# Low parts of the weights on DVE instead of POOL, and three more turns in a routing phase

## The chip, the cores and the metric

One core of a Trainium2 chip. The metric is the device time in microseconds of one execution; the number given is the median of several.

## What is computed

The reference chains three parts on float32 data.

```
state_t = gamma_h * state_{t-1} + k_t v_t^T          # per batch and head, 768 steps
y_t = (q_t . state_t) / sqrt(64)                     # decayed linear attention, 4 x 8 heads
x = y as 3072 tokens x 512
logits = x @ w_gate                                  # 8 experts, at most 384 tokens each
for (token, e) by falling logit:                     # greedy, over all 24576 pairs
    if token is free and expert e has room: assign
h = relu(x[e's tokens] @ w1[e]) @ w2[e]              # 512 -> 1024 -> 512
out = softplus(h @ w_in) @ w_out                     # 512 -> 2048 -> 512
```

The assignment is exact: which token goes to which expert depends on the order of all logits.

## The kernel before

The order of the instructions on each engine is written out by hand: each engine runs its instructions in the order in which the program emits them, and waits on the others by semaphores.

Up to about 203 us `Attn` computes the attention in 24 chunks of 128 tokens, and `Conv` turns the second network's weights, kept as 64-bit numbers, into float32 parts on DVE. Then `Ffn.start` runs routing phase 0, and `Ffn.emit` the feed-forward work of eight experts.

**Matmuls.** Every float32 product is made of three matmuls on rounded high parts and low parts: high times high, low times high, high times low (`mm3`). So each operand is split. `split_w` (L599) splits a 128x512 weight tile: ScalarE copies `raw` to `whi` with rounding (L604), and L605 subtracts it from `raw`, which gives `wlo`. There are 256 such tiles, 128 from `wraw` (w1 and w2 of the chosen experts, loaded by SP's queue) and 128 from `wo`. `whi` and `wlo` have rings of six buffers, `weights` (L788) keeps four tiles ahead of their use. Activations are split on ScalarE and DVE: `h1h`/`h1l` (L611, L612), `x2h`/`x2l` (L614, L615), `gh`/`gl` (L696, L697).

**Steps.** `plan` (L734) lists the steps of an expert: eight M1 (first layer, a block of 128 of 1024 hidden units, twelve matmuls), eight M2 (second layer), sixteen F1 (first layer of the second network), sixteen F2, and three `xt`, which transpose the next expert's token rows. M1, M2 and F1 have twelve matmuls 384 columns wide, F2 nine of 512. An F1 ends in three ScalarE operations (`sp`) and `gf` on DVE (L683); the `gl` made from it is needed two steps later by F2.

**Turns.** Routing goes expert by expert: phase i (`Route.phase`, L393) finds the expert that is filled next and the list of its tokens, and runs beside the matmuls of the experts before it. It is a generator; each `yield` ends a turn. `emit` (L767) calls for every step `weights`, then the step, then, on every step while the next list isn't there, else on every second one, one turn by `route` (L804). A phase starts with `top` (L354), which takes for each token its best remaining expert. Then come three levels of 46, 46 and 32 thresholds, each counted twice (coarse, fine): `compare` on DVE makes `G` (L378), two turns later `count` (L383) adds it up by 24 small matmuls (L385), DVE makes `ind` of it (L431), one turn later TensorE spreads it (L437), and DVE makes `satj` and the next base from that (L440, L446). Behind the levels come the counts `rs` (L457, used two turns later by the matmul of L464), the expert's number (turn "expert"), one-hot tiles `ohq` (L511) that begin with `tot` (L492), and the token list (turn "list"). If F1 with f = 10 comes before the next list is there, the loop at L779 runs all missing turns at once. `fetch_x` (L626) then gathers the next expert's rows by DMAs that POOL issues.

**Start.** In `start` (L816) the first two weight tiles are split in the turn of the first `ohq` of phase 0, the next two right behind the list.

Of the kernel before, what the change touches and what calls it, by code (L numbers as in the profile page):

```python
# [9 lines left out]
FT = mybir.dt.float32  # L10
# [6 lines left out]
OP = mybir.AluOpType  # L17
# [263 lines left out]
class Route:  # L281
# [72 lines left out]
    def top(self, c0, c1, first):  # L354

        v, E, n = self.nc.vector, self.E, c1 - c0
        s = slice(c0, c1)
        lm, m, aed, ik, sg = self.lm[:, s], self.m[:, s], self.aed[:, s], self.ik[:, s], self.sg[:, s]
        src = self.L[:, s]
        if not first:  # L360
            v.tensor_tensor(lm, src, self.pen[:, None, :].to_broadcast([128, n, E]), op=OP.add)
            src = lm
            v.tensor_scalar(self.u[:, s], self.asg[:, s], 0.0, None, op0=OP.is_equal)
        v.tensor_reduce(m, src, axis=AX.X, op=OP.max)
        v.tensor_tensor(lm, src, self.bc(m, n, E), op=OP.is_equal)
        v.tensor_scalar(m, m, 0.0, None, op0=OP.add)
        v.tensor_tensor(lm, lm, self.desc[:, None, :].to_broadcast([128, n, E]), op=OP.mult)
        v.tensor_scalar(sg, m.bitcast(I32), 31, 0x7fffffff, op0=OP.arith_shift_right, op1=OP.bitwise_and)
        v.tensor_reduce(aed, lm, axis=AX.X, op=OP.max)
        v.tensor_tensor(ik, m.bitcast(I32), sg, op=OP.bitwise_xor)  # L370
        v.tensor_tensor(self.oe[:, s], lm, self.bc(aed, n, E), op=OP.is_equal)
        v.tensor_scalar(sg, ik, 21, None, op0=OP.arith_shift_right)
        v.scalar_tensor_tensor(self.kf[:, s], sg, 1025.0, self.u[:, s], op0=OP.add, op1=OP.mult)
        v.tensor_scalar(self.kx[:, s], self.bc(self.kf[:, s], n, 2), -1.0, None, op0=OP.add)
# [12 lines left out]

    def first_part(self, c0, c1):

        self.top(c0, c1, True)  # L390
        self.compare(c0, c1, self.t0, 46)

    def phase(self, i, slow=True):  # L393
        nc, N, E, w = self.nc, self.N, self.E, self.wp
# [2 lines left out]
        gap = range  # L397
        last = i == E - 1
        if i:
            self.top(0, N, False)  # L400
        base = self.zero
        ps = None
        if last:
# [1 line left out]
        for l, (J, s1, sh, span) in enumerate(() if last else LEVELS):  # L405
            if l:
                lo = T([128, N], I32, "lo")
# [159 lines left out]
class Ffn:  # L567
# [31 lines left out]
    def split_w(self, key):  # L599
        nc = self.nc  # L600
        raw = self.wout[key[2]] if key[0] == "wo" else self.raws.pop(key)
        hi = self.ring.tile([128, 512], FR, name="whi")
        lo = self.ring.tile([128, 512], FR, name="wlo")
        nc.scalar.activation(hi, raw, AF.Copy)  # L604
        nc.gpsimd.tensor_sub(lo, raw, hi.bitcast(FT))  # L605
        self.ws[key] = hi, lo

    def split_act(self, ps, hi, lo, relu=False):
# [303 lines left out]
```

## Time and profile before

| what | us |
|---|---|
| median of three runs | 1120.59 (1120.57 to 1124.83) |
| the profiled execution | 1123.62 |
| its span (first to last instruction) | 1121.5 |
| TensorE busy | 1020.8 |
| DVE busy | 689.1 |
| ScalarE busy | 535.1 |
| POOL busy | 442.3 |

The page lists busy times by engine and by line of code; PE is TensorE, PEld its weight loads, ACT ScalarE. A row of a timeline gives the start of an instruction from the span's start, its duration, engine, line and operands, and in brackets the idle time before it with what ended that. Instructions of an engine may overlap by their start-up, so a row's duration can be somewhat longer than its distance to the next row.

### The profile page before, as it was taken

What the parts mean: (1) busy time and instruction counts of PE and PEld (TensorE: products, weight loads), DVE (VectorE), ACT (ScalarE), POOL (GpSimd) and SP (SyncE); (2) the same over time, 40 slices, a digit from 0 to 9 for tenths busy, and PEclk for the clock granted to TensorE, in tenths of its full rate; (3) what the DMA queues carried; (4) which work ended last, traced back from release to release, by engine and by line L of the source; (5) the groups of instructions that cost most, each with busy time, mean ns of one, the idle gap of its engine ahead of it and who ended that gap; (6) DMA issues with size and microseconds to landing.
All of it is one profiled execution on the core that took longest, in us unless ns stands there. A gap on an engine that the chain in (4) does not pass through costs nothing.

```text
span 1121.5 us, 18513 instructions
## 1 busy us (share of the span) xinstructions
PE 1020.8 (91%) x7041; PEld 922.8 (82%) x7041; DVE 689.1 (61%) x1510; ACT 535.1 (48%) x1041; POOL 442.3 (39%) x386
## 2 busy tenths in 40 slices
PE   5877874489999999999999999999999999999997
PEld 5776763378878988898889888988888899989996
DVE  5999999755765656467646665865586622441332
ACT  2444332224554465436543654365536654664663
POOL 4323320333335424542355235523452454337422
PEclk9888886589999999999999999999999999999999
DMA  8887873320113201320122012301220222013000
GB/s 317 302 284 263 301 228 104 104 75 1 39 38 105 65 1 38 95 75 1 39 81 90 1 38 76 94 1 30 75 67 1 76 85 85 1 47 122 1 1 29
DMA packets 38873, 97.51 MB, mean 87 GB/s; under 512 B 5120, under 2 KB 5248, under 8 KB 38784
## 3 DMA queue, kind: packets, MB, share of 16 engines
q1 hardware_dynamic: 34128, 83.11, 23.1%
q0 software_dynamic: 3840, 12.59, 3.4%
q8 instruction: 55, 0.90, 0.3%
q10 hardware_dynamic: 816, 0.63, 0.2%
q14 instruction: 34, 0.28, 0.1%
HBM read 83.73 MB, written 12.58 MB: 86 GB/s over the span
## 4 chain that ended last, share of the span: by engine, by line
PE 68%; DVE 23%; issue 3%; ACT 2%; DMA 2%; POOL 1%; SPq 0%; ACTq 0%; POOLq 0%; DVEq 0%
PE h L619 11%; PE h L621 10%; PE h L620 10%; PE acc L717 8%; PE acc L719 7%; PE acc L718 7%; PE acc L619 3%; PE acc L621 3%; PE acc L620 3%; PE rt L385 2%; DVE at L121 2%; DVE cM L233 2%; DVE cX L247 2%; DVE cX L251 2%; DVE base L446 1%
## 5 line engine op out<-in xcount | busy, mean ns | idle before, releaser
L605 POOL TENSOR_TENSOR wlo<-wo,whi 128x512 fp32r<-128x512 f32 x128 | 169.2, 1327 | 357.9 <-ACT whi L604 325.4
L605 POOL TENSOR_TENSOR wlo<-wraw,whi 128x512 fp32r<-128x512 f32 x128 | 164.1, 1302 | 189.6 <-ACT whi L604 172.3
L683 DVE SCALAR_TENSOR_TENSOR gf<-h,sp 128x384 f32<-128x384 f32 x128 | 71.2, 557 | 179.0 <-ACT sp L681 178.9
L619 PE MATMUL h<-x2h,wih 128*128 128x384 f32 x512 | 176.8, 345 | 0.0
L621 PE MATMUL h<-x2l,wih 128*128 128x384 f32 x512 | 173.2, 338 | 0.2 <-DVE x2l L615 0.2
L620 PE MATMUL h<-x2h,wil 128*128 128x384 f32 x512 | 173.4, 339 | 0.0
L717 PE MATMUL acc<-whi,gh 128*128 128x512 f32 x384 | 154.8, 403 | 0.0
L719 PE MATMUL acc<-whi,gl 128*128 128x512 f32 x384 | 152.5, 397 | 2.2 <-DVE gl L697 2.2
L718 PE MATMUL acc<-wlo,gh 128*128 128x512 f32 x384 | 152.0, 396 | 0.0
L679 ACT ACTIVATE sp<-h 128x384 f32<-128x384 f32 x128 | 62.4, 488 | 150.3 <-PE h L621 148.9
L697 DVE TENSOR_TENSOR gl<-gf,gh 128x384 fp32r<-128x384 f32 x128 | 103.4, 807 | 39.9 <-ACT gh L696 39.8
L611 ACT ACTIVATE h1h<-h 128x384 fp32r<-128x384 f32 x64 | 31.4, 491 | 170.7 <-PE h L621 170.7
L612 DVE SCALAR_TENSOR_TENSOR h1l<-h,h1h 128x384 fp32r<-128x384 f32 x64 | 35.3, 555 | 115.6 <-ACT h1h L611 115.6
L619 PEld LDWEIGHTS h<-x2h,wih 128*128 128x128 f32 x512 | 96.1, 188 | 4.1
L620 PEld LDWEIGHTS h<-x2h,wil 128*128 128x128 f32 x512 | 96.2, 188 | 3.0
L621 PEld LDWEIGHTS h<-x2l,wih 128*128 128x128 f32 x512 | 96.1, 188 | 0.8 <-DVE x2l L615 0.8
L619 PE MATMUL acc<-h1h,whi 128*128 128x384 f32 x256 | 89.7, 350 | 0.0
L719 PEld LDWEIGHTS acc<-whi,gl 128*128 128x128 f32 x384 | 72.4, 189 | 21.0 <-DVE gl L697 4.3
L619 PE MATMUL h<-xh,whi 128*128 128x384 f32 x256 | 89.0, 348 | 0.7 <-ACT xh L614 0.7
L696 ACT ACTIVATE gh<-gf 128x384 fp32r<-128x384 f32 x128 | 67.1, 524 | 46.5 <-DVE gf L683 39.0
L621 PE MATMUL acc<-h1l,whi 128*128 128x384 f32 x256 | 87.4, 341 | 0.0
L620 PE MATMUL acc<-h1h,wlo 128*128 128x384 f32 x256 | 87.2, 341 | 0.0
(197 smaller groups left out, 2047.4 us busy)
## 6 DMA issues: line engine op xcount, KB each, us to landing
wraw<-in_moe_w_dram SPq DMA_DIRECT2D x128, 256.0 KB, 2.7
qk_t<-in_qk_dram SPq DMA_DIRECT2D x24, 512.0 KB, 6.8
kv_t<-in_kv_dram SPq DMA_DIRECT2D x24, 512.0 KB, 5.5
raw<-in_moe_w_in_dram SPq DMA_DIRECT2D x16, 512.0 KB, 5.3
raw<-in_moe_w_out_dram SPq DMA_DIRECT2D x16, 512.0 KB, 4.7
xd<-xs SPq DMA_DIRECT2D x24, 256.0 KB, 6.0
gqt<-in_gqt_dram SPq DMA_DIRECT2D x5, 256.0 KB, 6.6
ctab<-in_tab_dram ACTq DMA_DIRECT2D x1, 536.0 KB, 5.7
```

The lines of the kernel that those rows point to most:

```text
L605: nc.gpsimd.tensor_sub(lo, raw, hi.bitcast(FT))
L612: nc.vector.scalar_tensor_tensor(lo, ps, 0.0, hi.bitcast(FT), op0=OP.max, op1=OP.subtract)
L619: nc.tensor.matmul(ps, wh, ah, start=start, stop=False)
L620: nc.tensor.matmul(ps, wl, ah, start=False, stop=False)
L621: nc.tensor.matmul(ps, wh, al, start=False, stop=stop)
L679: nc.scalar.activation(a, ps, AF.Abs)
L683: nc.vector.scalar_tensor_tensor(g, ps, 0.0, a, op0=OP.max, op1=OP.add)
L696: nc.scalar.activation(gh, g, AF.Copy)
L697: nc.vector.tensor_tensor(gl, g, gh.bitcast(FT), op=OP.subtract)
L717: nc.tensor.matmul(ps, gh[:, s], wh, start=f == 0, stop=False)
L718: nc.tensor.matmul(ps, gh[:, s], wl, start=False, stop=False)
L719: nc.tensor.matmul(ps, gl[:, s], wh, start=False, stop=f == 15)
```

## The change

The subtraction that makes `wlo` is issued on DVE instead of POOL, at the same place of the program. And `top` becomes a generator: for the phases in the loop it ends a turn behind the masked logits, a second one behind the best expert's index, and `phase` ends a third one behind `top`, ahead of the first `compare`. Phase 0's `first_part` runs it through without turns.

```diff
@@ top
             v.tensor_scalar(self.u[:, s], self.asg[:, s], 0.0, None, op0=OP.is_equal)
+            yield
         v.tensor_reduce(m, src, axis=AX.X, op=OP.max)
...
         v.tensor_reduce(aed, lm, axis=AX.X, op=OP.max)
+        if not first:
+            yield
         v.tensor_tensor(ik, m.bitcast(I32), sg, op=OP.bitwise_xor)
@@ first_part
-        self.top(c0, c1, True)
+        for _ in self.top(c0, c1, True):
+            pass
@@ phase
         if i:
-            self.top(0, N, False)
+            yield from self.top(0, N, False)
+            yield
@@ split_w
         nc.scalar.activation(hi, raw, AF.Copy)
-        nc.gpsimd.tensor_sub(lo, raw, hi.bitcast(FT))
+        nc.vector.tensor_tensor(lo, raw, hi.bitcast(FT), op=OP.subtract)
```

## Rows read from the trace of the kernel before

**Rows 1.** the head of the page: busy time, share of the span, instructions of each engine.

```profile
PE 1020.8 (91%) x7041; PEld 922.8 (82%) x7041; DVE 689.1 (61%) x1510; ACT 535.1 (48%) x1041; POOL 442.3 (39%) x386
```

**Rows 2.** the span cut into stretches: busy time of PE, PEld, DVE, ACT, POOL; clock; DMA.

```profile
216.00:320.00 104.00, 96.13 (x618) 87.13 (x619) 63.20 (x145) 44.84 (x88) 37.12 (x29) 0.93 0.14 41
...
880.00:1100.00 220.00, 220.00 (x1184) 205.41 (x1183) 78.43 (x122) 124.64 (x243) 97.40 (x84) 1.00 0.16 48
```

**Rows 3.** whom TensorE waited for, 216 to 880 us: total, times, longest.

```profile
PE rt L385 <- DVE G L378: 11.1, 7, 4.9
PE rt L464 <- DVE rs L457: 3.6, 3, 1.6
PE acc L719 <- DVE gl L697: 2.2, 3, 1.1
```

**Rows 4.** the stretches of low granted clock, in the same columns.

```profile
227.20:234.10 6.90, 4.23 (x34) 4.15 (x34) 3.86 (x9) 0.00 (x0) 1.49 (x2) 0.51 0.29 88
...
264.80:268.20 3.40, 3.40 (x12) 2.96 (x11) 1.55 (x4) 1.47 (x3) 0.00 (x0) 0.50 0.00 0
...
322.80:326.20 3.40, 3.11 (x29) 2.64 (x30) 2.60 (x6) 0.05 (x1) 1.26 (x1) 0.50 0.26 63
```

**Rows 5.** groups by line and shape: count, busy us, mean ns, idle time before.

```profile
L605 POOL TENSOR_TENSOR wlo<-wo,whi 128x512 fp32r<-128x512 f32 x128 | 169.2, 1327 | 357.9 <-ACT whi L604 325.4 <-PE acc L718 13.1 <-PE rt L437 10.9
...
L697 DVE TENSOR_TENSOR gl<-gf,gh 128x384 fp32r<-128x384 f32 x128 | 103.4, 807 | 39.9 <-ACT gh L696 39.8
...
L446 DVE TENSOR_TENSOR base<-ksat 128x1 f32<-128x1 f32 x21 | 23.1, 1099 | 0.7
...
L260 DVE TENSOR_TENSOR wo<-cM,cX 128x512 f32<-128x512 f32 x16 | 13.5, 845 | 0.3
```

**Rows 6.** timeline near the end, POOL and DVE: start us, us taken, operation.

```profile
1101.95 1.29 POOL L605 TENSOR_TENSOR wlo<-wo,whi 128x512 fp32r<-128x512 f32 x1 [2.91 <-ACT whi L604]
...
1102.54 1.12 DVE L697 TENSOR_TENSOR gl<-gf,gh 128x384 fp32r<-128x384 f32 x1 [0.59 <-ACT gh L696]
...
1106.74 0.56 DVE L697 TENSOR_TENSOR gl<-gf,gh 128x384 fp32r<-128x384 f32 x1 [0.59 <-ACT gh L696]
```

**Rows 7.** timeline of the first phase in the loop, DVE and PE.

```profile
222.05 1.27 DVE L363 TENSOR_SCALAR unas<-asg 128x24 f32<-128x24 f32 x1
...
227.54 1.19 DVE L373 SCALAR_TENSOR_TENSOR kf<-sg,unas 128x24 f32<-128x24 int32 x1
...
229.87 1.08 PE L385 MATMUL rt<-G,oe 128*8 128x46 bf16 x24 [4.88 <-DVE G L378]
```

**Rows 8.** timeline of the start, DVE and POOL.

```profile
195.02 0.16 DVE L446 TENSOR_TENSOR base<-ksat 128x1 f32<-128x1 f32 x1
...
196.47 0.69 DVE L260 TENSOR_TENSOR wo<-cM,cX 128x512 f32<-128x512 f32 x1
197.08 0.69 DVE L233 SCALAR_TENSOR_TENSOR cM<-cM,cX 128x512 f32<-128x512 f32 x1
...
200.90 0.14 DVE L492 COPY tot<-pS 128x1 f32<-128x1 f32 x1
...
202.47 0.56 DVE L511 TENSOR_TENSOR ohq<-io,px 128x768 bf16<-128x768 bf16 x1
...
203.32 2.56 POOL L605 TENSOR_TENSOR wlo<-wraw,whi 128x512 fp32r<-128x512 f32 x2 [42.20 <-ACT whi L604]
...
203.39 1.36 DVE L517 TENSOR_TENSOR rh<-dd,cidb 128x144 bf16<-128x144 f32 x1
204.67 2.56 DVE L511 TENSOR_TENSOR ohq<-io,px 128x768 bf16<-128x768 bf16 x3
```

**Rows 9.** timeline of a change of level, DVE and PE.

```profile
259.02 1.17 DVE L446 TENSOR_TENSOR base<-ksat 128x1 f32<-128x1 f32 x1
...
263.66 0.76 PE L385 MATMUL rt<-G,oe 128*8 128x32 bf16 x24 [1.43 <-DVE G L378]
```

**Rows 10.** timeline, DVE, the four `x2l` of one expert.

```profile
840.64 1.95 DVE L615 TENSOR_TENSOR x2l<-acc,x2h 128x384 fp32r<-128x384 f32 x4
```

## Prediction

> **What bounds the kernel now.** I read the head of the page first, then the span cut into stages, then TensorE's waits and granted clock, and last the DVE timeline around each of those waits. TensorE is busy for 91% of the span, DVE 61%, POOL 39% [rows 1]. That is an average over stages with different limits. Up to about 203 us DVE makes the attention and the weights' conversion, and the change touches nothing there (`first_part` runs the same operations in the same order). From 216 us on the feed-forward work runs on TensorE: 880 to 1100 us, where no routing is left, it is busy for 220.00 of 220.00 us; the same kind of work with routing beside it, 216 to 320 us, shows 96.13 of 104.00 [rows 2]. So what can be won lies in the holes between 216 and 880 us. They are listed [rows 3]: TensorE waited 11.1 us for the compare `G`, 3.6 for `rs` and 2.2 for `gl`, together 16.9 us, and all of it for DVE.
>
> Some holes cost a second time. The granted clock is 0.5 (1.2 GHz) in 227.2 to 234.1, 264.8 to 268.2 and 322.8 to 326.2 us, the first two in or right behind waits for `G` [rows 7, 9]; TensorE was busy for 4.23, 3.40 and 3.11 us in them [rows 4]. At 2.4 GHz that work takes half, so the low clock cost (4.23 + 3.40 + 3.11) / 2 = 5.4 us. Waits and clock together are 22.3 us.
>
> **Why DVE is late there.** POOL's `wlo` takes 1.33 us, 128 times from `wo`, and as long from `wraw`. On DVE the mean `gl` took 807 ns and the `base` addition, one element a partition, 1099 ns [rows 5]. Two `gl` of one shape show why: one beside a POOL `wlo` (1101.95 to 1103.24) took 1.12 us and ended as that `wlo` had; one with POOL idle took 0.56 us [rows 6]. The same holds of small operations: of the thirteen that `top` issues, four took over 1.1 us in the first phase in the loop, from 1.27 at 222.05 to 1.19 at 227.54, the last of the four [rows 7]. With those four, `G` was ready only after TensorE had stood for 4.88 us [rows 7]. So a `wlo` on POOL holds DVE operations that run beside it until it is done.
>
> **The change, part by part.** *The 256 low parts on DVE.* The trace has no `wlo` on DVE. Its nearest row is L260, a two-input 128x512 f32 operation from SBUF with POOL idle (POOL's first `wlo`, at 203.32, follows 42.20 us without work): 0.69 us, the next one starting 0.61 us behind it [rows 8]. The other end is the 845 ns mean of L260, taken mostly beside POOL work [rows 5]. I take 0.61, since POOL does no elementwise work in this stage any more. 256 x 0.61 = 156 us more on DVE, against at least 128 x (0.807 - 0.56) = 32 us from `gl` and 21 x (1.10 - 0.16) = 20 us from `base` (0.16 us with POOL idle, at 195.02 [rows 8]). DVE goes from 689 to at most 793 us, some 72% of the new span: below its limit on average, so its total costs nothing. What counts is where a `wlo` stands in DVE's queue. `weights` is called ahead of a step's matmuls and `route` behind them, so a `wlo` stands behind the routing of the step before and ahead of this step's `h1l` or `gf`, which wait for TensorE and ScalarE anyway. Its own input `whi` (ScalarE) stands in the same place of ScalarE's queue.
>
> Does a turn still fit? The tightest regular ones are the compares at a change of level: `base` started at 259.02 and the count that needs `G` began at 263.66. `base` took 1.17 us where it takes 0.16 with POOL idle, and two operations on `kf` behind it were held as long [rows 8, 9]. Without POOL the turn takes 4.6 - 3.0 = 1.6 us and ends at 260.6. TensorE could have used it at 262.1 (263.66 less the 1.43 us that it waited, less some latency [rows 9]). That leaves about 1.5 us of air, more than one `wlo`. So I cost these waits at nothing afterwards; the cover is the two steps of matmuls between a compare and its count (4.20 us for two, the distance of the two `gl` [rows 6]), and without it each would cost what it costs now.
>
> *Three more turns.* `top` is spread over three turns, and the compare comes in the fourth. In the first phase, which takes one turn a step, TensorE then has three more steps (6.3 us) of matmuls ahead of the first count. That wait was 4.9 of the 11.1 us [rows 3, 7]; it goes by the turns alone, even if POOL still held DVE. The turns add no instruction. They do move the rest: a phase's `list` comes with its 32nd turn instead of the 29th. Counted through the plan, phase 1 lists at step 32, and the loop that would drain it stands ahead of the F1 step with f = 10, step 35; later phases have more to spare. So no burst, and the gather's issue on POOL (no longer behind a `wlo`) keeps its place. SP's expert read comes three turns later and is still some ten steps ahead of its loads.
>
> *What is late next.* Turns now meet other steps. Counted the same way, the turn with the first `ohq` (behind a product that needs TensorE) falls on the M2 step with f = 5 in phase 5 and with f = 6 in phase 6, just ahead of the four `x2l`, which the first F1 needs. From `tot` to the end of the first `ohq` and `rh` is 200.90 to about 203.6 us, 2.7 us [rows 8]; four `x2l` take 1.95 us, so the first 0.5 [rows 10]. Phase 6: 0.4 (latency) + 2.7 + 0.61 (`wlo`) + 0.5 = 4.2 us behind the end of that M2, while F1 wants it one step and two matmuls later, 2.1 + 0.35 = 2.45: a new wait of 1.8 us. Phase 5: 0.4 + 2.7 + 0.61 + 1.5 (three `ohq`) + 0.61 + 0.5 = 6.3 against 4.2 + 0.35: again 1.8. Together 3.5 us. Elsewhere turns that fall on a transpose step, or a `gl` behind a heavy turn, keep some tenths each: I allow 2.0 us, bounds 0 and 4.
>
> *The start.* Ahead of 216 us the chain runs through DVE. The `rh` that took 1.36 us beside the first `wlo` should take 0.2, the three `ohq` 1.5 (one ahead of them took 0.56) for 2.56; two `wlo` of 0.61 enter between them [rows 8]. 203.39 + 0.2 + 1.2 + 1.5 = 206.3 for 207.2: 0.9 us sooner, and the list, the gather and the first matmul with it.
>
> *The sum*, from the profiled execution: 1123.6 us outside, 1121.5 span. 1123.6 - 16.9 - 5.4 - 0.9 + 3.5 + 2.0 = 1105.9. That execution is 3.0 us above the median of 1120.59; on that scale the sum is 1102.9. I can't tell from one trace whether those 3 us lie in the waits that go, so I take 1104, between the two.
>
> **The rivals.** *DVE stays late (half).* A `wlo` of 0.61 us takes the place of a hold of about 1.1 in DVE's line, and about half of the 22.3 us stays: 1123.6 - 11.2 - 0.9 + 2 = 1113. For it speaks that DVE is in order and the routing chain is short of air at some places; against it, that the `wlo` stands behind the routing turn and the 1.5 us of air.
>
> *Nothing moves.* The whole hold returns as `wlo` time, if two of them stood in each critical turn: 1123.6 - 0.9 = 1122.7, on the median's scale 1120. The Trainium skill ("Perfetto Trace Analysis", section "Optimizing Scalar/DVE Operations") says that shifting work between VectorE and GpSimd may not help, as they share a read port; by that rule the time stays at 1120.6, and no run shown here has the work on DVE. The rows speak against it: POOL holds DVE [rows 6], but a two-input operation of this size takes 0.61 us on DVE against 1.33 on POOL [rows 5, 8], and with POOL empty it holds nobody else.
>
> *Slower.* A `wlo` waits in DVE's line for its `whi`, and the routing behind it waits too; on POOL that wait harmed nobody. It decides once `whi` comes more than the 1.5 us of air late at a compare. Six compares in six phases, 36, each late by 0.8 us beyond it, are 29 us: 1106 + 29 = 1135. Against it: `whi` stands in ScalarE's line where its producer's work has ended about when DVE's has.
>
> **How the numbers follow.** Forecast 0.70 (1104), half 0.17 (1113), nothing 0.08 (1120), slower 0.05 (1135). The range reaches from every wait gone with no new one (1123.6 - 23.2 - 3.0 = 1097) to past the half case: 1096 to 1115. About 0.5%, 5.6 us, is what a measurement tells from no change, so faster (below 1115) is 0.70 + 0.17 = 0.87, same 0.08, slower 0.05.
>
> **What would show it.** Right: `gl` and `base` at 0.56 and 0.16 us throughout; `wlo` on DVE at 0.7 us x256; no wait for `G` at the first count of the first phase; full clock from about 220 us on; TensorE's waits for DVE between 216 and 880 us below 8 us, the largest for `x2l` in the sixth expert's or the fifth's first F1; no `ind` or `satj` that TensorE waits for. Wrong: `wlo` on DVE near 0.85 us or idle DVE in front of `wlo` for `whi`; waits for `G` that have moved to later turns; low clock stretches that come back behind the `x2l` waits.

## The result, and the profile after

The changed kernel takes 1102.16 us (median of four runs, 1101.34 to 1103.90), the kernel before, run beside it, 1120.58 (1120.47 to 1124.83). The ratio is 0.9829, 95% interval 0.9803 to 0.9854: 18.4 us less. The forecast was 1104, within 1096 to 1115. The profiled execution took 1103.90 us, its span 1102.1.

First the head of the page of the changed kernel, which answers to [rows 1]:

```profile
PE 1010.4 (92%) x7041; PEld 915.5 (83%) x7041; DVE 700.3 (64%) x1766; ACT 535.3 (49%) x1041; POOL 110.5 (10%) x130
```

DVE took over 256 operations and is busy for only 11.2 us more than before. Where that comes from is in its groups by line and shape (busy us, mean ns of one, idle time before with its cause), which answer to [rows 5]. The diff moves line numbers: L697 is now L702, L446 is L451.

```profile
L610 DVE TENSOR_TENSOR wlo<-wo,whi 128x512 fp32r<-128x512 f32 x128 | 86.9, 684 | 0.0
L610 DVE TENSOR_TENSOR wlo<-wraw,whi 128x512 fp32r<-128x512 f32 x128 | 85.4, 685 | 4.8 <-ACT whi L609 4.8
L702 DVE TENSOR_TENSOR gl<-gf,gh 128x384 fp32r<-128x384 f32 x128 | 70.8, 553 | 11.9 <-ACT gh L701 11.9
L427 DVE TENSOR_SCALAR thr<-thrA,ksat 128x46 f16<-128x46 f32 x14 | 3.5, 247 | 0.5
L451 DVE TENSOR_TENSOR base<-ksat 128x1 f32<-128x1 f32 x21 | 3.3, 159 | 0.7
L363 DVE TENSOR_SCALAR unas<-asg 128x24 f32<-128x24 f32 x7 | 1.2, 171 | 0.0
```

The two `wlo` groups add 86.9 + 85.4 = 172.3 us. Everything else on DVE became 161.1 us shorter: `gl` fell from 807 to 553 ns, `base` from 1099 to 159 ns, `ohq`, `unas`, `thr` and others gave the rest. Those operations did not get smaller; nothing holds them any more. The last column matters as much: DVE stood idle in front of all 256 `wlo` for 4.8 us together, so they do not wait for `whi`.

Next, whom TensorE waited for from 216 to 880 us (total, times, longest), which answers to [rows 3]:

```profile
PE h L626 <- DVE x2l L620: 2.5, 2, 1.3
PE h L624 <- ACT xh L619: 0.7, 1, 0.7
PE acc L724 <- DVE gl L702: 0.4, 1, 0.4
```

`G` (11.1 us) and `rs` (3.6 us) are gone. `xh` stands ahead of the first feed-forward matmul and was there before too. `x2l` is new. Then the span cut into stretches, in the columns of [rows 2]:

```profile
216.00:320.00 104.00, 103.25 (x674) 92.98 (x673) 65.70 (x193) 51.56 (x101) 3.13 (x4) 0.97 0.14 41
221.60:1098.00 876.40, 869.99 (x5399) 789.46 (x5397) 502.63 (x1315) 460.56 (x897) 48.08 (x69) 1.00 0.16 50
221.60:880.00 658.40, 655.29 (x4258) 589.72 (x4257) 404.14 (x1139) 340.74 (x664) 35.48 (x49) 1.00 0.17 51
```

From 221.6 us on the granted clock is 1.00 until 1098 us, past the last matmul (1094.30); the three stretches of [rows 4] have no counterpart. In 216 to 320 us TensorE is busy for 103.25 us where it was for 96.13.

These two views close the account. The kernel before, in the same columns:

```profile
216.00:880.00 664.00, 645.62 (x4161) 579.40 (x4162) 407.35 (x936) 328.59 (x642) 275.45 (x231) 0.99 0.16 50
```

There TensorE was busy for 645.62 of the 664.00 us; less the 0.64 us before its first feed-forward matmul at 216.64, that is 17.7 us of holes. Now it is 658.40 - 655.29 = 3.1 us of holes. The holes gave 14.6 us and the clock 5.4 (as worked out in the prediction): 20.0 us together. The **feed-forward stretch**, from the start of the first M1 matmul to the start of the last matmul, went from 897.4 to 877.0 us: 20.4 us. The rest of the span went the other way: the first M1 starts at 217.33 us instead of 216.64.

For the experiments the stretch is the finer measure, because that start moves by itself: in fourteen profiled executions of kernels with the same attention part it lay between 214.9 and 218.7 us. Its first few microseconds still run at the low clock, for 3.4 to 5.9 us in the four executions of the changed kernel. One matmul of M1 starts 0.32 us behind the other there, 0.17 us at the full clock, so about half of that time is lost to the clock. Less that half, the four give 874.9, 874.7, 874.7 and 874.9 us, the kernel before 895.5. Below, "corrected stretch" means this number. It comes from one execution of each kernel, and the four repeats show how far to trust it (0.2 us).

### The profile page after: what moved, and what is told of

Its sections match the earlier page's. It is cut to its first block, busy times and chain, and to the rows that moved or that the text cites. A ratio compares the mean times of both kernels' runs of the same rounds, so it can differ in the third digit from the quotient of the medians.

```text
span 1102.1 us, 18357 instructions
## 1 busy us (share of the span) xinstructions
PE 1010.4 (92%) x7041; PEld 915.5 (83%) x7041; DVE 700.3 (64%) x1766; ACT 535.3 (49%) x1041; POOL 110.5 (10%) x130
## 4 chain that ended last, share of the span: by engine, by line
PE 71%; DVE 14%; issue 10%; DMA 3%; ACT 1%; POOL 1%; ACTq 0%; SPq 0%; POOLq 0%; DVEq 0%
PE h L624 12%; PE h L626 11%; PE h L625 11%; PE acc L722 7%; PE acc L724 7%; PE acc L723 7%; PE acc L624 4%; PE acc L626 3%; PE acc L625 3%; PE rt L388 2%; DVE cX L251 2%; DVE cX L247 2%; DVE at L121 2%; DVE cM L233 1%; DMA raw<-in_moe_w_in_dram 1%
## 5 line engine op out<-in xcount | busy, mean ns | idle before, releaser
L610 DVE TENSOR_TENSOR wlo<-wraw,whi 128x512 fp32r<-128x512 f32 x128 | 85.4, 685 | 4.8 <-ACT whi L609 4.8
L626 PE MATMUL h<-xl,whi 128*128 128x384 f32 x256 | 87.3, 341 | 0.0
L625 PE MATMUL h<-xh,wlo 128*128 128x384 f32 x256 | 87.1, 340 | 0.0
L724 PEld LDWEIGHTS acc<-whi,gl 128*128 128x128 f32 x384 | 72.3, 188 | 17.7 <-DVE gl L702 0.9
L610 DVE TENSOR_TENSOR wlo<-wo,whi 128x512 fp32r<-128x512 f32 x128 | 86.9, 684 | 0.0
```

The costliest lines, as they stand in the source:

```text
L610: nc.vector.tensor_tensor(lo, raw, hi.bitcast(FT), op=OP.subtract)
L625: nc.tensor.matmul(ps, wl, ah, start=False, stop=False)
L626: nc.tensor.matmul(ps, wh, al, start=False, stop=stop)
L724: nc.tensor.matmul(ps, gl[:, s], wh, start=False, stop=f == 15)
```

## The experiments

### The same kernel again, and each part alone

The changed kernel again, beside the parts of the change:

> The changed kernel once more, as the measure for the runs beside it. Both theories: 1102 us, 18 us below the kernel before. In its trace the first matmul of the feed-forward work tells whether the start, 0.7 us later than before in the first trace where 0.9 sooner was forecast, moves from run to run (then it comes between 214 and 217.5 us) or is always late by the gather (then the rows' DMA is issued about 1 us behind the index, again).

Measured: 1101.14 us (1100.71 to 1105.93), before 1123.11; ratio 0.9811 (0.9792 to 0.9830). And twice more, beside later experiments:

> The changed kernel beside it, for the comparison on one chip: 1101 to 1103 us, 877 us from the first feed-forward matmul to the last.

Measured: 1102.34 us, ratio 0.9826 (0.9806 to 0.9846).

> The changed kernel beside it, for the comparison on one chip: 1101 to 1103 us, 874.7 us in the stretch so corrected.

Measured: 1102.72 us (1101.80 to 1103.11), ratio 0.9822 (0.9800 to 0.9843). The gain is the same on four occasions.

**The low parts on DVE, without the turns.** The kernel before with one line changed:

```diff
-        nc.gpsimd.tensor_sub(lo, raw, hi.bitcast(FT))
+        nc.vector.tensor_tensor(lo, raw, hi.bitcast(FT), op=OP.subtract)
```

> The kernel before with the low parts on DVE, without the three turns. Theory (POOL held DVE, and DVE free of it is fast enough): the 13 operations of top take 3.4 us at 0.17 to 0.36 each, so the first count of the first phase waits some 1.5 us where it waited 4.9, that of the second about as long; the turns fall on the steps of before, so the two waits for x2l (1.3 us each in the changed kernel) are gone: 1101 to 1105 us, the same as the changed kernel. Rival (the turns carry a good part): the first counts wait 3 us and more, the low clock comes back behind them twice, 1108 us and above.

Measured: 1102.77 us (1101.81 to 1103.21), ratio 0.9822 (0.9804 to 0.9840); corrected stretch 874.4 us. TensorE's waits, 216 to 880 us:

```profile
PE rt L385 <- DVE G L378: 2.0, 2, 1.3
PE acc L719 <- DVE gl L697: 1.5, 2, 1.1
PE h L619 <- ACT xh L614: 0.7, 1, 0.7
```

This part alone gives the whole gain; of the 4.88 us at the first count [rows 7] 0.62 is left. Without the turns 2.0 us of `G` and 1.5 of `gl` stay; with them those go and 2.5 us of `x2l` come. The turns are worth nothing measurable here.

**The turns, with the low parts on POOL.** The changed kernel with that line put back:

```diff
-        nc.vector.tensor_tensor(lo, raw, hi.bitcast(FT), op=OP.subtract)
+        nc.gpsimd.tensor_sub(lo, raw, hi.bitcast(FT))
```

> The kernel before with the three turns, the low parts left on POOL. Theory: the first count of the first phase waits no more (4.9 us and 1 to 3.5 us of low clock gone), the waits at changes of level, for rs and for gl stay, some 8 us, and the holds make the new waits for x2l larger than 1.3 us: 1112 to 1117 us. Rival (the turns carry a good part): 1108 us and below.

Measured: 1109.23 us (1107.38 to 1112.04), ratio 0.9889 (0.9865 to 0.9913); corrected stretch 881.0 us. That lies between what the theory and its rival gave. TensorE's waits, and DVE's `gl` and `base` by group:

```profile
PE rt L388 <- DVE G L381: 4.0, 4, 2.9
PE h L626 <- DVE x2l L620: 2.2, 2, 1.5
PE rt L488 <- DVE mem L485: 0.5, 1, 0.5
PE acc L724 <- DVE gl L702: 0.4, 1, 0.4
```

```profile
L702 DVE TENSOR_TENSOR gl<-gf,gh 128x384 fp32r<-128x384 f32 x128 | 95.1, 743 | 35.6 <-ACT gh L701 35.6
L451 DVE TENSOR_TENSOR base<-ksat 128x1 f32<-128x1 f32 x21 | 18.5, 882 | 0.7
```

DVE's operations are still held, yet 7.1 of the 11.1 us of `G` waits are gone. In the kernel before, two of these waits stood at the first count of a phase, 4.88 us in phase 1 and 2.39 in phase 2; with the turns no first count waits, for there the turns give the late result more matmuls to hide behind. At the later counts the waits have moved and not shrunk (3.8 us before, 4.0 now). The waits for `rs` went as well, and in place of the three low-clock stretches of [rows 4] there is one, behind the 2.86 us wait; as every turn behind `top` falls on another step now, that may be the reason, but no run separates it. So the two parts are largely substitutes. On the corrected stretch the DVE move saves 21.1 us, the turns 14.5, both 20.7. Whoever adds up the parts would expect 35.6.

### Is it the holding?

**A shadow on POOL.** The changed kernel, and POOL does the same subtraction into a scratch tile that nobody reads:

```diff
         nc.vector.tensor_tensor(lo, raw, hi.bitcast(FT), op=OP.subtract)
+        nc.gpsimd.tensor_sub(self.ring.tile([128, 512], FT, name="shadow", bufs=2), raw, hi.bitcast(FT))
```

> The changed kernel, and POOL does the same subtraction again into a tile that nobody reads. DVE's own work is that of the changed kernel. Theory (POOL's reading holds DVE): gl goes back from 0.55 to about 0.8 us, base from 0.16 to about 1 us, wlo on DVE to 0.9 us and more, and TensorE's waits for DVE return: 1112 to 1122 us, more than with the turns alone, as DVE has the low parts besides. Rival (it was POOL's lateness with wlo, or its place in the order, and not the hold): 1102 us.

Measured: 1134.51 us (1132.14 to 1135.75), ratio 1.0103 (1.0079 to 1.0128), slower than the kernel before; corrected stretch 904.6 us. The direction was expected, the size was not. DVE's groups, then TensorE's waits:

```profile
L610 DVE TENSOR_TENSOR wlo<-wraw,whi 128x512 fp32r<-128x512 f32 x128 | 131.8, 1047 | 2.4 <-ACT whi L609 2.4
L703 DVE TENSOR_TENSOR gl<-gf,gh 128x384 fp32r<-128x384 f32 x128 | 106.3, 831 | 11.9 <-ACT gh L702 11.9
L610 DVE TENSOR_TENSOR wlo<-wo,whi 128x512 fp32r<-128x512 f32 x128 | 103.9, 816 | 0.0
L451 DVE TENSOR_TENSOR base<-ksat 128x1 f32<-128x1 f32 x21 | 15.9, 757 | 0.7
```

```profile
PE rt L388 <- DVE G L381: 13.2, 6, 4.2
PE h L627 <- DVE x2l L621: 6.8, 3, 4.3
PE rt L442 <- DVE ind L436: 2.4, 5, 0.9
PE rt L488 <- DVE mem L485: 1.6, 2, 0.8
```

POOL's work delays nobody by its result, and still DVE's operations with two inputs in SBUF, the memory of the tiles, are held again, `wlo` itself (1047 and 816 ns for 685) included. Those with one input in PSUM, where the matmuls write, are not: `gf` takes 557 ns here, in the kernel before and in the changed one, and `h1l` and `x2l` stay at about 550. The waits for `G` are back, 13.2 us in all, turns or no turns, and the low clock comes back in four stretches, two in or behind a wait for `G` and two in or behind one for `x2l`. The kernel now pays for `wlo` on DVE and for the hold; the expectation named both and gave them too little.

**POOL busy, but writing.** The changed kernel, and behind each `wlo` POOL copies a small piece of `whi` (so that it starts at the same moment) and then fills a scratch tile:

```diff
+        near = self.ring.tile([128, 128], FT, name="near", bufs=1)
+        fill = self.ring.tile([128, 1024], FT, name="fill", bufs=1)
+        nc.gpsimd.tensor_copy(near, hi[:, 0:128].bitcast(FT))
+        nc.gpsimd.memset(fill, 0.0)
```

> The changed kernel, and POOL, behind each high part, copies 128x128 and then only writes: a memset of 128x1024, about 1 us, into a tile that nobody reads. By the shadow run POOL's subtraction, which reads twice and writes, holds DVE. Theory A (what holds DVE is POOL's reading): DVE operations with two inputs in SBUF are free of it, gl at 0.55 to 0.6 and base at 0.16 to 0.3 us, only single-input ones (unas, kf, thr) may be held; time within 5 us of the changed kernel. Theory B (any elementwise work of POOL holds DVE): gl at 0.75 us, base at 0.7 and the time above 1112 us.

Measured: 1105.40 us (1104.47 to 1105.88), ratio 0.9851 (0.9814 to 0.9889); corrected stretch 877.1 us. The groups of POOL and DVE:

```profile
L614 POOL MEMSET fill<- 128x1024 f32 x256 | 243.8, 953 | 0.0
L610 DVE TENSOR_TENSOR wlo<-wraw,whi 128x512 fp32r<-128x512 f32 x128 | 88.4, 708 | 4.8 <-ACT whi L609 4.8
L706 DVE TENSOR_TENSOR gl<-gf,gh 128x384 fp32r<-128x384 f32 x128 | 73.2, 572 | 11.9 <-ACT gh L705 11.9
L427 DVE TENSOR_SCALAR thr<-thrA,ksat 128x46 f16<-128x46 f32 x14 | 11.3, 804 | 0.5
L451 DVE TENSOR_TENSOR base<-ksat 128x1 f32<-128x1 f32 x21 | 3.8, 183 | 0.7
```

POOL is busy no shorter per tile than with a subtraction (953 + 476 ns for 1327 [rows 5]), and `gl`, `wlo` and `base`, all with two inputs, are nearly free of it. What is left goes with the copy, which reads: the 19 `gl` that ran beside a memset alone took 0.55 us on average, the 33 that ran beside the copy too 0.63. So it is not POOL being busy that holds these; it is POOL reading. `thr`, a `tensor_scalar`, was held (804 ns for 247), and five `kx`, of the same kind, took 0.68 to 0.86 us for 0.19 beside the memset alone. The Trainium skill ("SBUF — State Buffer", section "Who interferes with whom") says that a DVE operation with two inputs in SBUF contends with a POOL instruction that reads there and not with one that only writes, and that `tensor_scalar` can enter a mode that takes the shared ports whole; the two kernels agree with both. The hold of such operations has its price: where `lo`, `kf`, `kx` and `thr` of one turn took 1.6 to 2.0 us each, one wait for `G` came back.

```profile
PE rt L388 <- DVE G L381: 1.5, 1, 1.5
```

### Is DVE short of time?

The rival "half" said that a `wlo` on DVE takes a place in its line that the routing needs. So DVE does every low part twice, the second time into a scratch tile:

```diff
         nc.vector.tensor_tensor(lo, raw, hi.bitcast(FT), op=OP.subtract)
+        nc.vector.tensor_tensor(self.ring.tile([128, 512], FT, name="shadow", bufs=2), raw, hi.bitcast(FT), op=OP.subtract)
```

> The changed kernel, and DVE makes every low part twice, the second time into a tile that nobody reads: 256 more operations of 0.61 us, 156 us of DVE. Theory (DVE has air of about 1.5 us at its tightest regular turns, so only the places that are late already pay): the two waits for x2l, 1.3 us each, grow by 0.6 and 1.2, some turns of tenths appear; from the first feed-forward matmul to the last 880 to 884 us against 877 in the changed kernel, 1104 to 1109 us in all. Rival (DVE's line is short all along, a low part takes the place of a hold): 890 us and more, 1115 us and above.

Measured: 1108.60 us (1107.26 to 1109.89), ratio 0.9884 (0.9846 to 0.9922); corrected stretch 878.4 us. The head of its page, TensorE's waits, and the one stretch of low clock after 222 us:

```profile
PE 1012.7 (92%) x7041; PEld 916.6 (83%) x7041; DVE 845.9 (77%) x2022; ACT 535.8 (48%) x1041; POOL 116.0 (10%) x130
```

```profile
PE h L627 <- DVE x2l L621: 4.3, 2, 2.4
PE h L625 <- ACT xh L620: 0.7, 1, 0.7
PE acc L725 <- DVE gl L703: 0.7, 2, 0.4
```

```profile
709.80:713.20 3.40, 3.40 (x12) 3.40 (x11) 2.23 (x5) 0.34 (x1) 0.00 (x0) 0.50 0.00 0
```

DVE is busy for 146 us more and the stretch grows by 3.6 us: 1.8 more in the two `x2l` waits and, with 3.40 us of work at half speed, 1.7 for the clock. No `G` wait came. So DVE has air in nearly every turn, and the rival "half" falls. The air that the prediction worked out for a change of level, 1.5 us, held two `wlo` of 0.6.

### The new waits for `x2l`

The prediction said that the first `ohq` turn falls ahead of the `x2l` in phases 5 and 6. To test it, the turn is left for later there:

```diff
+            if fn == self.m2 and i and f in (5, 6):
+                continue
             if self.listed <= i + 1 or step % 2 == 0:
```

> The changed kernel, where from the second expert on the steps M2 with f = 5 and f = 6 take no turn, so that no routing stands ahead of the four x2l. Theory (the first ohq and what stands behind tot make x2l late in phases 5 and 6): both waits for x2l are gone, 2.5 us, and the gl wait of 0.4 moves; from the first feed-forward matmul to the last 874 us against 877, 1098 to 1100 us in all. Rival (x2l waits for something else, the low parts or ScalarE): the waits stay, 877 us.

Measured: 1102.47 us (1099.84 to 1104.32), ratio 0.9827 (0.9798 to 0.9856); stretch 874.4 us, with no low clock in it to correct for, so 0.3 to 0.5 less than the 874.7 to 874.9 of the changed kernel. TensorE's waits:

```profile
PE rt L493 <- DVE tb L490: 2.8, 3, 1.1
PE h L624 <- ACT xh L619: 0.7, 1, 0.7
```

The cause is shown: without that turn no `x2l` is late. But the time stays nearly the same, because the turns behind it moved to F1 steps and a wait for `tb`, an input of the next small matmul, came three times. (The expected 874 us for the uncorrected stretch came out only because this execution had the full clock from the start; less low clock, the gain is a few tenths and not the 3 us forecast.) So `tb` was given one turn more ahead of its matmul, in the phases of the loop; the line in `start` below belongs to the next test.

```diff
         v.tensor_copy(tb, ps[0:48, 400:401].to_broadcast([48, 128]))
-        for _ in gap(1):
+        for _ in gap(1 + (i > 0)):
             yield
@@ emit
+            if fn == self.m2 and i and f in (5, 6):
+                continue
@@ start, behind the first two weight tiles
+                        awake = self.ring.tile([128, 128], FT, name="awake", bufs=1)
+                        self.nc.gpsimd.tensor_copy(awake, self.ws[self.keys[1]][1][:, 0:128].bitcast(FT))
```

> The kernel of e9_skip_awake with one more turn behind tb in the phases of the loop. Skipping the turns ahead of x2l took those two waits away and put three others in their place, 2.8 us for tb where its turn falls on an F1 step, so the stretch kept its length. Theory (each is the distance in turns between a DVE result and the matmul that needs it): with two turns behind tb no wait above 0.4 us for DVE is left between the first and the last feed-forward matmul; that stretch, less half of the time at the low clock at its head, is 871.5 us against 874.7, and the whole some 3.5 us shorter than the changed kernel, 1097 to 1099 us. Rival (the wait moves on again): 874 to 875 us.

Measured: 1097.46 us (1096.76 to 1099.25), ratio 0.9780 (0.9758 to 0.9801), against 1102.72 us (1101.80 to 1103.11) of the changed kernel beside it; corrected stretch 870.4 us. From 221.6 to 880 us TensorE has next to no hole left:

```profile
221.60:880.00 658.40, 658.22 (x4274) 592.13 (x4272) 404.10 (x1134) 343.96 (x670) 34.93 (x49) 1.00 0.17 52
```

This beats both kernels: 5.3 us less than the change, of which 4.5 lie in the corrected stretch. The turn behind `tb` was not run without the other two edits; the kernel with those two alone, below, has 874.0, so the turn is worth 3.6 of them on top.

### The start

Phase 0's chain on DVE got shorter as forecast, but part of that was lost again behind it. At the list of phase 0, POOL's timeline of the changed kernel (start us, us taken; its `ix`, the index that the gather needs, began on DVE at 208.06):

```profile
209.18 1.29 POOL L636 DMA_INDIRECT rows<-xd,ix  x1 [46.89 <-DMA wraw<-in_moe_w_dram]
```

In the kernel before `ix` began at 207.84 and the gather at 208.30: 0.46 us, now 1.12. POOL had done nothing for 46.89 us, where before it had made `wlo`. (The releaser in the brackets is inferred; the gather needs no `wraw`.) The chain of the changed kernel's profile shows the time: two steps of POOL's queue for that line stand behind `ix`, with time behind each in which POOL waited for nothing that the profile shows.

```profile
208.30 0.04 POOLq L636
208.35 0.61 issue
208.96 0.02 POOLq L636
208.97 0.21 issue
```

So POOL was given one small copy right ahead of it:

```diff
                         self.weights(2)
+                        awake = self.ring.tile([128, 128], FT, name="awake", bufs=1)
+                        self.nc.gpsimd.tensor_copy(awake, self.ws[self.keys[1]][1][:, 0:128].bitcast(FT))
```

> The changed kernel with one copy of 128x128 on POOL behind the second low part, some 2 us ahead of the token list of phase 0. Theory (POOL, idle for 46.9 us, is slow to issue its first gather: 1.1 to 1.3 us behind the index in three runs with POOL idle, 0.45 to 0.65 in three with work on it): the gather is issued about 0.6 us sooner behind the index, and from the index to the first feed-forward matmul it takes 9.0 instead of 9.6 us; the whole is 0.6 us shorter, below what the total can tell. Rival (the gather waits for something else that has moved): 1.1 us and more again.

Measured: 1102.29 us (1100.91 to 1102.84), ratio 0.9821 (0.9783 to 0.9859). POOL's timeline:

```profile
204.91 0.41 POOL L844 COPY awake<-wlo 128x128 f32<-128x128 f32 x1 [43.98 <-issue]
207.27 1.35 POOL L636 DMA_INDIRECT rows<-xd,ix  x1 [1.95 <-DVE ix L534]
```

The gather starts 0.45 us behind `ix` again (the queue's steps for its line now run ahead of `ix`, at 204.92 and 205.00), and from `ix` to the first M1 it is 8.8 us instead of 9.3 to 9.5. Together with the skipped turns:

```diff
+            if fn == self.m2 and i and f in (5, 6):
+                continue
@@ start
+                        awake = self.ring.tile([128, 128], FT, name="awake", bufs=1)
+                        self.nc.gpsimd.tensor_copy(awake, self.ws[self.keys[1]][1][:, 0:128].bitcast(FT))
```

> The changed kernel with both mends: no turn on the M2 steps with f = 5 and 6 from the second expert on, and the copy on POOL ahead of the first gather. Theory: 874.4 us from the first feed-forward matmul to the last (877 in the changed kernel) and 8.8 us from the index to the first one (9.5): 3 us less than the changed kernel beside it, 1098 to 1100 us. Rival: the stage ahead of the routing, which moves by 3 us from run to run, hides it; then the two lie within 1.5 us of each other in all, and only the stretches of the trace tell them apart.

Measured: 1101.22 us (1100.41 to 1104.32), ratio 0.9824 (0.9806 to 0.9842), beside 1102.34 of the changed kernel; corrected stretch 874.0. That is short of what was expected: the skipped turns mostly move a wait, as above, and half a microsecond at the start can be seen in the trace and not in the total.

## Why the prediction was right, point by point

**The mechanism.** Right. That POOL's subtraction holds DVE was read from two `gl` of one shape [rows 6]; the shadow kernel brings the hold and waits for `G` back, and the filling kernel shows that operations with two inputs are held where POOL reads and not where it only writes. The prediction's "holds DVE operations that run beside it" is too wide: those with an input in PSUM (`gf`, `h1l`, `x2l`) were never held. Forecast `gl` 0.56 and `base` 0.16 us, measured 0.553 and 0.159; forecast `wlo` 0.61 us apart at 0.69 duration, measured 0.684.

**The waits and the clock.** Right and a little low. All of `G` and `rs` went; of `gl` 0.4 us stays. The 5.4 us of low clock went. In two other kernels a low stretch began right behind a wait: 2.40 us for `x2l` (the low parts twice) and 2.86 us for `G` (the turns alone). The changed kernel, whose longest wait is 1.34 us, has none; as the 1.43 us of [rows 9] had one behind it, while waits of 2.96 and 2.77 us for `G` in the shadow kernel had none, no border can be read from these.

**The new waits for `x2l`.** Right in cause, phase and step; 1.8 us each was forecast. DVE's timeline in phase 6, then TensorE's:

```profile
816.94 0.16 DVE L497 COPY tot<-rt 128x1 f32<-128x1 f32 x1 [1.57 <-PE rt L494]
...
819.45 0.31 DVE L522 TENSOR_TENSOR rh<-dd,cidb 128x144 bf16<-128x144 f32 x1
819.68 0.68 DVE L610 TENSOR_TENSOR wlo<-wo,whi 128x512 fp32r<-128x512 f32 x1
820.28 1.94 DVE L620 TENSOR_TENSOR x2l<-acc,x2h 128x384 fp32r<-128x384 f32 x4
```

```profile
820.88 0.45 PE L626 MATMUL h<-x2l,wih 128*128 128x384 f32 x1 [1.34 <-DVE x2l L620]
```

From `tot` to the end of `rh` it took 2.8 us, then `wlo`, then `x2l`, in the order of the prediction. The wait is 1.34 us here and 1.20 in phase 5. The term was 3.5 and measured 2.5. In phase 6 the chain was sized right, if not in its parts (4.14 us from the end of the M2 at 816.74 to the waiting matmul, forecast 4.2; the 0.4 of latency in it was 0.2), but TensorE came to need `x2l` only 2.80 us behind that end, for 2.45.

**"Tenths elsewhere".** 2.0 us allowed, within 0 to 4; the holes that are left, 3.1 us with `x2l`, leave about 0.6 for it. This and `x2l` are 2.4 us of the 3.9 by which the stretch beat its sum (16.8 us less forecast, 20.7 measured, both corrected); another 0.8 are old holes that were not in the list of waits (17.7 against 16.9); the last 0.7 have no name.

**The start.** Half wrong, and it failed in one step. DVE's part, from phase 0's first `base` to `ix`, fell from 25.9 to 25.0 us, the 0.9 forecast. What failed is "the list, the gather and the first matmul with it": I had checked that no queue stands in the gather's way, and not how long POOL would take to issue it after 47 us without work. That took back 0.5 to 0.7 us. In the profiled execution the first M1 even came 0.7 us later than before; the rest of that is the movement of the attention part from run to run.

**DVE's total.** "At most 793 us" held, at 700.3. The two groups that I had priced gave 52.4 us; other held operations gave twice as much.

**The turns.** "It goes by the turns alone, even if POOL still held DVE" is right: with the turns alone no first count waits, neither in phase 1 nor in phase 2. The turns alone are worth some 12 us (1.1% of 1120.6; 14.5 on the corrected stretch), far more than that one wait. What the prediction did not say is that on top of the other part they bring nothing: it counted the `G` waits once, so the sum was not harmed, but a reader could take the turns for a part of the gain. They cost their own `x2l` waits.

**The rivals.** "Half" and "slower" fall with the low parts done twice (no `G` wait at 846 us of DVE) and with the 4.8 us of idle time in front of `wlo`. "Nothing moves" falls with the result: the same subtraction takes 0.685 us on DVE against 1.33 on POOL and freed 161 us of other DVE time. The warning of the Trainium skill ("Perfetto Trace Analysis", section "Optimizing Scalar/DVE Operations") that such a shift might not help did not come true here.

**Between 1104 and 1102.2.** On the profiled execution the sum was 1105.9 and the time 1103.9: the stretch 3.9 us better, the start 1.6 worse and its clock 0.2. The two errors run against each other, so part of the closeness is luck. The open question whether the 3.0 us above the median lay in the waits stays open; the value between the two stood 1.1 us above the lower one, 1102.9.

## What to carry to other kernels

Before giving an engine more work, look at what the engine that now does it costs its neighbour: two operations of one shape, one beside it and one alone, show it. Two cures for the same wait need not add up, so price them together and count the wait once. A turn that is moved lands on some other step; count which, and give the result behind it one step more of matmuls, as 4.5 of the last 5.3 us here came from that.

## What the runs showed of the hardware

- An indirect DMA that POOL issued after some 47 us without work started later. In seven executions where POOL had been idle so long, the gather began 1.10 to 1.12 us behind the start of its index; in seven where it had worked some 3 us before or less, 0.45 to 0.46. One copy of 0.41 us, 2 us ahead, is enough. Whether the idle time itself does it is not shown: with the copy, steps of POOL's queue that otherwise stand behind the index run ahead of it.
- A `memset` on POOL, with a short copy ahead of it, hardly touched DVE operations with two inputs (`gl` 572 ns for 553, `base` 183 for 159), but it held small `tensor_scalar`s (`thr` 804 ns for 247).
- A small operation is held as long as a large one: an addition of one element a partition took 1099 ns on average in the kernel with POOL's subtractions and 159 without them.
- DVE operations with one input in PSUM were not held by POOL's subtractions: `gf` took 557 ns with them and without.
